# An FFT convolution with routed experts on one core: transposes as row tiles, a new order of a stage, and two moved constants

## The chip, the core and the metric

The kernel runs on one core of one Trainium2 chip. A core has TensorE (matmuls and transposes, into PSUM banks), VectorE, ScalarE, GpSimd and SyncE, which here only issues DMAs. Each engine works through a queue of its own in order. The metric is device time in microseconds of one execution; the times given are medians of runs.

## What is computed

Four sequences of 11456 rows with 128 channels go through a long convolution, done as a transform of length 5760 = 90 x 64, a product and the transform back. Each row of the result is then sent to one of eight experts.

```python
u = x * v
y = irfft(rfft(u) * rfft(filter))[:S]        # per sequence and channel
x = (x * y).reshape(B * S, D)                # 45824 rows of 128
logits = x @ w_gate + modality_bias[modality_id]
e = argmax(logits); gate = softmax(logits)[e]
out = gate * (relu(x @ w1[e]) @ w2[e])       # e of that row
```

## The kernel before

The work is a list of stages on a time line that is written out by hand. For each sequence there is an outer stage and a middle stage in turn. An outer stage has 16 steps (`q`). In one step it transforms the last sequence back (`turn`, `inverse`), routes rows of it (`half`, `logits`, `lturn`, `biased`, `choice`, `send`, `store`, `places`), and transforms the next one forward (`load`, `product`, `forward`). The middle stage multiplies the spectra. After four sequences the last outer stage has no forward part, and then the experts run, which is the second half of the time.

The string `OUTER` gives the order within a step for the first three outer stages, and a delay in steps for each part: `half:2` in step t works on q = t - 2. `LAST` is the same for the last outer stage. TensorE, ScalarE, VectorE and SyncE take their instructions in just this order. Routing parts other than `half` run in every second step, so two steps make one round: one with `lturn`, `biased` and `choice`, one with `logits` and `send`.

What the prediction's steps touch:

- `turn` (L693, L694) transposes A, [128, 90] at a time, to [90, 128]; four transposes fill a PSUM bank, and ScalarE copies the bank to `w_t`. Two blocks a step, so 16 transposes and four copies.
- `inverse` (L702 to L708): eight matmuls from `w_t` into a `pair` buffer, a copy of half of it by ScalarE (L705), then a sum, a difference and a product with x on VectorE (L706, L707, L708), which writes `xo`.
- `forward` (L494, L497): two halves of 32 matmuls in tiles of 64 x 64, each into a `pair` buffer that ScalarE copies to A. There are two `pair` buffers for `forward` and `inverse` together.
- `product` (L479, L482, L483) on VectorE makes what `forward` reads one step later.
- `half` (L751, L753): eight transposes of [109, 128] and two copies by ScalarE, for the logits (L759, L761), which `lturn` (L766) transposes back.
- `choice` (L780 to L801) on VectorE, with one exponential by ScalarE (L784): maximum, one-hot of the expert, a running count, the gate weight and the token's number. L790 adds a large constant where a position holds no row, so that no expert is chosen there.
- `send` (L819 to L833): counts by three small matmuls, then the row's place. L833 adds the same constant, so that a scatter drops the row.
- `store` (L810) writes `xo` to DRAM; there are three `xo` buffers.
- `send_rows` (L275) scatters rows by GpSimd, a few at a time, each paced by an instruction of VectorE.

Of the kernel before, what the change touches and what calls it, by code (L numbers as in the profile page):

```python
# [47 lines left out]
def surely_full(n):  # L48
# [7 lines left out]
NOWHERE = 1 << 20  # L56
OUTER = ("turn0:0 turn1:0 lturn:3 biased:3 half:2 product:0 forward:1 choice:3 "
         "inverse:0 logits:2 send:4 load_x:-1 load:-2 store:4 places:5")
# [36 lines left out]
def shape_constants():  # L95
# [32 lines left out]
    order = lambda a: a.reshape(D, 2, NO, 2, 4).transpose(0, 2, 4, 1, 3).reshape(D, NO * NC)  # L128
    first = (E - np.arange(E))[None, :, None] * np.ones((D, 1, NC))
    keep = np.ones((D, E, NC))  # L130
# [3 lines left out]
    small = np.concatenate([  # L134
        order(tok)[:, 0:NC], order(~there)[:, 0:NC] * 2.0 ** 22,
        first.reshape(D, E * NC), keep.reshape(D, E * NC), tri,
# [36 lines left out]
_at = 0  # L173
for _name, _n in (("tok", NC), ("bad", NC), ("first", E * NC), ("keep", E * NC),
                  ("tri", D), ("ones", D), ("reg", E), ("iota", NF)):
    SMALL[_name] = (_at, _at + _n)
    _at += _n
# [4 lines left out]
def hyena_moe_kernel(ctx: ExitStack, tc: tile.TileContext, a: dict, out: bass.AP,  # L182
# [24 lines left out]
    def sm(name):  # L207
        lo, hi = SMALL[name]
        return small[:, lo:hi]
# [147 lines left out]
    def first_table(new):  # L357

        n1 = new("n1", [1, E])
        dve.tensor_sub(n1, base1[0:1], reg)  # L360
        yield
        yield from floor_div(new, n1, n1, T, 0)
        yield from tile_table(new, tab1, used, reg, n1, NW1, T)
# [3 lines left out]
    with ExitStack() as cv:  # L367
# [35 lines left out]
        def split_constants():  # L403
            dve.tensor_copy(base, sm("reg"))
            dve.tensor_copy(both, small[:, SMALL["tri"][0]:SMALL["ones"][1]])
# [48 lines left out]
        def xo_of(b, o):  # L454

            return xo_t[(NO * b + o) % NXO]
# [222 lines left out]
        def inverse_stages(b):  # L679
# [8 lines left out]

            def turn(q, blk):
                for c in range(2):  # L690
                    p = bank("wt")
                    for j in range(4):
                        pe.transpose(p[0:N1, D * j:D * j + D], A[:, blk, :, 8 * q + 2 * j + c], ident)  # L693
                    act.copy(w_t[q % 2][blk][:, c], p[0:N1])  # L694

# [42 lines left out]
        def route_stages(b):  # L738
# [4 lines left out]
            fst = sm("first")[0:PU].rearrange("p (e c) -> p e c", e=E)  # L743
            bad_of = lambda o: sm("bad")

            def turn(o, half):
                xo = xo_of(b, o)
                for way in range(2):
                    pt = bank("xT")
                    for h in range(4):  # L750
                        pe.transpose(pt[:, PU * h:PU * h + PU], xo[0:PU, way, half, h, 0:D],  # L751
                                     ident[0:PU, 0:PU])
                    act.copy(xT_t[:, 2 * way + half].rearrange("p h n -> p (h n)"),  # L753
                             pt[:, 0:4 * PU])

# [19 lines left out]
            def choice(o):  # L775
# [13 lines left out]
                dve.tensor_reduce(mb, ec(sco), axis=AX.X, op=ALU.max)  # L789
                dve.tensor_add(mb, mb, bad_of(o)[0:PU])  # L790
                dve.tensor_tensor(oh[0:PU], sco, wide(mb), op=ALU.is_equal)
                dve.tensor_tensor_scan(
# [6 lines left out]
                by_h = lambda t: t.rearrange("p (h g) -> p h g", h=4)  # L799
                dve.reciprocal(xov[:, :, :, D], by_h(se))  # L800
                s = dve.tensor_scalar_add(xov[:, :, :, D + 1].bitcast(I32), by_h(sm("tok")[0:PU]),  # L801
                                          float(b * S + 8 * o))
                paced(s)

# [9 lines left out]
            def send(o):  # L814
# [12 lines left out]
                dve.tensor_add(base, base, pn)  # L827
                paced(dve.tensor_mul(ro, ro, oh[0:PU]))
                sl = rt.tile([PU, NC], F32, tag="sl", name="sl")
                dve.tensor_reduce(sl, ec(ro), axis=AX.X, op=ALU.add)  # L830
                ix = ix_t[i % 2]
                by_h = lambda t: t.rearrange("p (h g) -> p h g", h=4)
                dve.tensor_add(ix[0:PU].rearrange("p (g h) -> p h g", h=4), by_h(sl), by_h(bad_of(o)[0:PU]))  # L833

# [111 lines left out]
    def rest():  # L946


        assert not waiting
        sp.dma_start(pad, a["c_pad"].rearrange("p (j r) -> p j r", j=TH // D))  # L950
        sp.dma_start(xs[E * R:E * R + TH, :].rearrange("(p j) r -> p j r", j=TH // D), pad)
        end = new("end", [1, E], I32)
        dve.tensor_copy(end, base[0:1])
        yield
        for e in range(E):
            v = nc.values_load(
                end[0:1, e:e + 1], engines=[ENG.SP], min_val=0, max_val=E * R - TH,
                skip_runtime_bounds_check_because="a region holds every token and a tile more")
            after_all(sp.dma_start(xs[ds(v, TH), :].rearrange("(p j) r -> p j r", j=TH // D), pad),
                      scatters)  # L960
            yield

    def later_tables():

        nall, full, start, left = (new(n, [1, E]) for n in ("nall", "full", "start", "left"))
        dve.tensor_sub(nall, base[0:1], reg)
        yield
# [301 lines left out]
```

## Time and profile before

| | |
|---|---|
| time, median of 3 runs | 2077.25 us (2075.55 to 2083.45) |
| the profiled execution, its own time | 2075.4 us |
| its span, first to last instruction | 2073.5 us |
| TensorE (PE) busy | 1954.0 us, 94% |
| VectorE (DVE) busy | 1761.6 us, 85% |
| ScalarE (ACT) busy | 1277.9 us, 62% |
| GpSimd (POOL) busy | 1165.5 us, 56% |
| mean granted TensorE clock | 0.985 |

Shares are means over stages that differ: the outer stages, the middle stages and the experts have different limits. In the rows below PE is a matmul or a transpose and PEld the load of its stationary operand. A time in brackets is how long the engine stood idle ahead of the instruction, and behind the arrow is what it waited for. An entry such as x16 says that so many instructions in a row are shown as one line, with the time from the first's start to the last's end. Shapes are partitions x elements, and 64*128 in front of them is the tile of TensorE that is used. Matmul ends are modelled.

### The profile page before, as it was taken

Reading aid. Unit: us, or ns where it says so; the run is one execution under the profiler, and the core shown is the slowest. Engines: PE = TensorE matmul, PEld = TensorE weight load, DVE = VectorE, ACT = ScalarE, POOL = GpSimd, SP = SyncE. Lnnn points to the kernel's source line nnn. Section 1 sums busy time; section 2 is a strip of 40 time slices with the busy share of each in tenths; the row PEclk is TensorE's granted clock in tenths of the full one; section 3 lists DMA queues with packets and bytes.
Section 4 is the critical chain, followed back from the end, with each engine's and each line's share of the span. In section 5 each row is a group of like instructions: output and inputs, shape, how many; then the busy total and the mean of one; then the engine's idle time right before and its main releaser. Section 6 shows DMA issues by size and latency. Waiting matters only on the chain. (4 is left out here: it accounts for less than half of the span.)

```text
span 2073.5 us, 50275 instructions
## 1 busy us (share of the span) xinstructions
PE 1954.0 (94%) x17646; PEld 1549.2 (75%) x17646; DVE 1761.6 (85%) x2708; ACT 1277.9 (62%) x2372; POOL 1165.5 (56%) x1054
## 2 busy tenths in 40 slices
PE   8899898999989998999799999999999999999997
PEld 8688565776667665776477888887888888888897
DVE  6599899999999899997678988897888888888886
ACT  5555675457735675446466666665666666666675
POOL 0144004765668566974456677786556555555654
PEclk9999999999999999999899999999999999999998
DMA  8565678879988898856798466664655555555421
GB/s 320 183 190 174 232 270 263 280 265 310 331 257 260 283 334 285 280 191 175 186 248 223 90 132 136 130 125 106 116 99 96 100 97 97 97 100 98 88 44 29
DMA packets 610842, 379.47 MB, mean 183 GB/s; under 512 B 424026, under 2 KB 542005, under 8 KB 610585
## 3 DMA queue, kind: packets, MB, share of 16 engines
q1 hardware_dynamic: 587193, 328.62, 58.5%
q0 software_dynamic: 23104, 47.34, 6.6%
q8 instruction: 141, 2.31, 0.5%
q14 instruction: 116, 0.95, 0.2%
q10 hardware_dynamic: 288, 0.25, 0.1%
HBM read 272.75 MB, written 103.70 MB: 182 GB/s over the span
## 5 line engine op out<-in xcount | busy, mean ns | idle before, releaser
L1097 ACT ACTIVATE hh<-ph 128x512 fp32r<-128x512 f32 x724 | 433.6, 599 | 320.8 <-PE ph L1094 316.5
L1098 DVE SCALAR_TENSOR_TENSOR hl<-ph,hh 128x512 fp32r<-128x512 f32 x724 | 487.9, 679 | 161.3 <-ACT hh L1097 153.4
L275 POOL DMA_INDIRECT xs<-back,to x360 | 401.7, 1116 | 327.9 <-DVE se L796 109.7
L1163 POOL DMA_INDIRECT out<-ot,x x362 | 373.0, 1030 | 160.2 <-issue 36.8
L1092 PE MATMUL ph<-xh,wh 128*128 128x512 f32 (+1 forms) x792 | 297.4, 376 | 8.0 <-ACT wh L1063 8.0
L1094 PE MATMUL ph<-xl,wh 128*128 128x512 f32 (+1 forms) x792 | 296.0, 374 | 9.0 <-POOL xl L1080 9.0
L1118 PE MATMUL po<-hl,wh 128*128 128x512 f32 (+1 forms) x792 | 295.7, 373 | 1.0 <-DVE hl L1098 0.8
L1093 PE MATMUL ph<-xh,wl 128*128 128x512 f32 (+1 forms) x792 | 295.0, 373 | 0.0
L1116 PE MATMUL po<-hh,wh 128*128 128x512 f32 (+1 forms) x792 | 294.9, 372 | 0.0
L1117 PE MATMUL po<-hh,wl 128*128 128x512 f32 (+1 forms) x792 | 294.6, 372 | 0.0
L672 ACT COPY A<-pw 128x512 f32<-128x512 f32 (+1 forms) x184 | 97.1, 579 | 186.9 <-PE pw L668 186.9
L1080 POOL TENSOR_TENSOR xl<-xT,xh 128x512 fp32r<-128x512 f32 (+1 forms) x77 | 96.2, 1249 | 200.8 <-ACT xh L1076 200.8
L624 PE MATMUL pz<-A,work 128*64 128x256 f32 x1440 | 182.7, 397 | 10.4 <-DMA work<-in_c_to 7.1
L668 PEld LDWEIGHTS pw<-work 64*128 64x128 f32 x2856 | 166.3, 189 | 30.5 <-ACT work L606 19.2
L637 POOL TENSOR_TENSOR work<-work 128x512 f32<-128x512 f32 (+1 forms) x92 | 115.3, 1254 | 128.3 <-DVE work L633 127.6
L668 PE MATMUL pw<-work 64*128 64x128 f32 x2856 | 180.2, 278 | 2.9 <-POOL work L654 2.6
L1094 PEld LDWEIGHTS ph<-xl,wh 128*128 128x128 f32 x792 | 149.7, 189 | 36.9 <-POOL xl L1080 10.8
L1092 PEld LDWEIGHTS ph<-xh,wh 128*128 128x128 f32 x792 | 149.9, 189 | 33.5 <-ACT wh L1063 8.3
L1118 PEld LDWEIGHTS po<-hl,wh 128*128 128x128 f32 x792 | 149.6, 189 | 30.1 <-DVE hl L1098 4.8
L1093 PEld LDWEIGHTS ph<-xh,wl 128*128 128x128 f32 x792 | 149.9, 189 | 26.0 <-DVE wl L1064 0.4
L1117 PEld LDWEIGHTS po<-hh,wl 128*128 128x128 f32 x792 | 149.7, 189 | 25.7
L1116 PEld LDWEIGHTS po<-hh,wh 128*128 128x128 f32 x792 | 149.7, 189 | 25.3
(183 smaller groups left out, 3618.9 us busy)
## 6 DMA issues: line engine op xcount, KB each, us to landing
work<-hs SPq DMA_DIRECT2D x66, 512.0 KB
work<-in_x SPq DMA_DIRECT2D x64, 512.0 KB
work<-in_xd SPq DMA_DIRECT2D x58, 512.0 KB
work<-in_v SPq DMA_DIRECT2D x51, 512.0 KB
xr<-xo SPq DMA_DIRECT2D x64, 365.6 KB
back<-xr SPq DMA_DIRECT2D x120, 195.0 KB
work<-in_c_to SPq DMA_DIRECT2D x88, 256.0 KB
blocks<-xs SPq DMA_DIRECT2D x328, 64.0 KB
```

What stands on the lines that cost most here:

```text
L275: s = pool.indirect_dma_start(out=xs, out_offset=bass.IndirectOffsetOnAxis(ap=ix, axis=0), in_=src, in_offset=None, bounds_check=E * R - 1 ...
L624: pe.matmul(z[64 * s:64 * s + 64, t, r], k["b"][:, t, s, r], A[:, :, 4 * g + 2 * t + s], start=True, stop=True)
L668: pe.matmul(v[s][:, t, blk], k[of][at, t, r, blk], k["c"][at, t, r], start=i == 0, stop=i == len(terms) - 1)
L1092: pe.matmul(p, k[0, "h"][:, f:f + D], k["xh"], start=True, stop=False)
L1093: pe.matmul(p, k[0, "l"][:, f:f + D], k["xh"], start=False, stop=False)
L1094: pe.matmul(p, k[0, "h"][:, f:f + D], k["xl"], start=False, stop=True)
L1097: act.activation(hh, ph, AF.Relu)
L1098: steps.append(ins_of(dve.scalar_tensor_tensor(hl, ph, 0.0, hh.bitcast(F32), op0=ALU.max, op1=ALU.subtract)))
L1116: pe.matmul(po, k[1, "h"][:, f], hh[:, t], start=g == 0, stop=False)
L1117: pe.matmul(po, k[1, "l"][:, f], hh[:, t], start=False, stop=False)
L1118: pe.matmul(po, k[1, "h"][:, f], hl[:, t], start=False, stop=g == NCH - 1)
L1163: s = pool.indirect_dma_start(out=out, out_offset=bass.IndirectOffsetOnAxis(ap=ix, axis=0), in_=src, in_offset=None, bounds_check=N - 1, o ...
```

## The change

`turn` and `half` do each transpose in two: the upper 64 partitions and the rest, each in a row tile of TensorE of its own and into a PSUM bank of its own. A block now has 16 transposes of [64, 90] and a bank for each of the two tiles; the two copies by ScalarE take one bank each, that is, half of the columns of all results instead of all columns of half of them. `half` has 16 transposes, of 64 and 45 partitions.

In `OUTER`, `product` and `forward` come right behind the turns; `half` follows, and `lturn`, `biased` and `choice` come behind `half` instead of ahead of it. `LAST` stays.

A position without a row now has zeros in the constant `first`, and the comparison takes at least 0.5, so that nothing is chosen there: L790 and the constant `bad` go. The base of all places starts at 2^22 (`FAR`) and the chosen expert's place is that less 2^22, so that a minimum over the experts gives the place and, where none is chosen, a number beyond the end: L833 goes, and the reduction writes the place itself. Token numbers are written by ScalarE instead of L801.

```diff
@@ -54,7 +54,8 @@
 NH = (N - T * NF - E) // TH + E
 RW = D + 2
 NOWHERE = 1 << 20
-OUTER = ("turn0:0 turn1:0 lturn:3 biased:3 half:2 product:0 forward:1 choice:3 "
+FAR = float(1 << 22)
+OUTER = ("turn0:0 turn1:0 product:0 forward:1 half:2 lturn:3 biased:3 choice:3 "
          "inverse:0 logits:2 send:4 load_x:-1 load:-2 store:4 places:5")
 LAST = ("inverse:1 logits:3 turn0:0 half:2 lturn:3 turn1:0 biased:4 choice:4 load_x:-1 store:4 "
         "send:5 places:5")
@@ -126,13 +127,13 @@
     win = win.reshape(2, 64, 2, N2).transpose(2, 1, 3, 0)
 
     order = lambda a: a.reshape(D, 2, NO, 2, 4).transpose(0, 2, 4, 1, 3).reshape(D, NO * NC)
-    first = (E - np.arange(E))[None, :, None] * np.ones((D, 1, NC))
+    first = (E - np.arange(E))[None, :, None] * order(there * 1.0)[:, None, 0:NC]
     keep = np.ones((D, E, NC))
     keep[:, :, 0] = 0
     q, p = np.arange(D)[:, None], np.arange(D)[None, :]
     tri = np.concatenate([-(q >= p).astype(float), np.ones((D, D))], 1)
     small = np.concatenate([
-        order(tok)[:, 0:NC], order(~there)[:, 0:NC] * 2.0 ** 22,
+        order(tok)[:, 0:NC],
         first.reshape(D, E * NC), keep.reshape(D, E * NC), tri,
         np.ones((D, 1)) * (np.arange(E) * R)[None, :],
         np.ones((D, 1)) * np.arange(NF)[None, :],
@@ -171,7 +172,7 @@
 
 SMALL = {}
 _at = 0
-for _name, _n in (("tok", NC), ("bad", NC), ("first", E * NC), ("keep", E * NC),
+for _name, _n in (("tok", NC), ("first", E * NC), ("keep", E * NC),
                   ("tri", D), ("ones", D), ("reg", E), ("iota", NF)):
     SMALL[_name] = (_at, _at + _n)
     _at += _n
@@ -357,7 +358,7 @@
     def first_table(new):
 
         n1 = new("n1", [1, E])
-        dve.tensor_sub(n1, base1[0:1], reg)
+        dve.scalar_tensor_tensor(n1, base1[0:1], -FAR, reg, op0=ALU.add, op1=ALU.subtract)
         yield
         yield from floor_div(new, n1, n1, T, 0)
         yield from tile_table(new, tab1, used, reg, n1, NW1, T)
@@ -401,7 +402,7 @@
                          .partition_broadcast(D).rearrange("p (m e) -> p m e", m=2))
 
         def split_constants():
-            dve.tensor_copy(base, sm("reg"))
+            dve.tensor_scalar_add(base, sm("reg"), FAR)
             dve.tensor_copy(both, small[:, SMALL["tri"][0]:SMALL["ones"][1]])
 
         pool.memset(wg, 0.0)
@@ -687,11 +688,16 @@
                 sp.dma_start(t, a["x"][b, q])
 
             def turn(q, blk):
+                p = [bank("wt")[0:N1].rearrange("p (i d) -> p i d", d=64) for _ in range(2)]
                 for c in range(2):
-                    p = bank("wt")
                     for j in range(4):
-                        pe.transpose(p[0:N1, D * j:D * j + D], A[:, blk, :, 8 * q + 2 * j + c], ident)
-                    act.copy(w_t[q % 2][blk][:, c], p[0:N1])
+                        for k in range(2):
+                            at = slice(64 * k, 64 * k + 64)
+                            pe.transpose(p[k][:, 4 * c + j], A[at, blk, :, 8 * q + 2 * j + c],
+                                         ident[at, at])
+                w = w_t[q % 2][blk].rearrange("p c (j k d) -> p (c j) k d", k=2, d=64)
+                for k in range(2):
+                    act.copy(w[:, :, k], p[k])
 
             def transform(q):
 
@@ -741,17 +747,19 @@
             ec = lambda t: t.rearrange("p e c -> p c e")
             wide = lambda t: t.unsqueeze(1).broadcast_to([PU, E, NC])
             fst = sm("first")[0:PU].rearrange("p (e c) -> p e c", e=E)
-            bad_of = lambda o: sm("bad")
 
             def turn(o, half):
                 xo = xo_of(b, o)
+                rows = (slice(0, 64), slice(64, PU))
+                pt = [bank("xT")[:, 0:8 * (at.stop - at.start)].rearrange("p (w h n) -> p w h n", w=2, h=4)
+                      for at in rows]
                 for way in range(2):
-                    pt = bank("xT")
                     for h in range(4):
-                        pe.transpose(pt[:, PU * h:PU * h + PU], xo[0:PU, way, half, h, 0:D],
-                                     ident[0:PU, 0:PU])
-                    act.copy(xT_t[:, 2 * way + half].rearrange("p h n -> p (h n)"),
-                             pt[:, 0:4 * PU])
+                        for p, at in zip(pt, rows):
+                            pe.transpose(p[:, way, h], xo[at, way, half, h, 0:D], ident[at, at])
+                xT = xT_t.rearrange("p (w s) h n -> p w s h n", w=2)[:, :, half]
+                for p, at in zip(pt, rows):
+                    act.copy(xT[:, :, :, at], p)
 
             def logits(o):
                 pl = bank("pl")
@@ -787,8 +795,8 @@
                 dve.scalar_tensor_tensor(sco, dl, 0.0, fst, op0=ALU.is_ge, op1=ALU.mult)
                 mb = rt.tile([PU, NC], F32, tag="mb", name="mb")
                 dve.tensor_reduce(mb, ec(sco), axis=AX.X, op=ALU.max)
-                dve.tensor_add(mb, mb, bad_of(o)[0:PU])
-                dve.tensor_tensor(oh[0:PU], sco, wide(mb), op=ALU.is_equal)
+                dve.scalar_tensor_tensor(oh[0:PU], sco, 0.5, wide(mb), op0=ALU.max,
+                                         op1=ALU.is_equal)
                 dve.tensor_tensor_scan(
                     sc[0:PU].rearrange("p e c -> p (e c)"), sm("keep")[0:PU],
                     oh[0:PU].rearrange("p e c -> p (e c)"), 0.0, op0=ALU.mult, op1=ALU.add)
@@ -797,10 +805,9 @@
                 dve.tensor_scalar_add(se, se, 1e-9)
                 xov = xo[0:PU].rearrange("p w s h r -> p h (w s) r")
                 by_h = lambda t: t.rearrange("p (h g) -> p h g", h=4)
-                dve.reciprocal(xov[:, :, :, D], by_h(se))
-                s = dve.tensor_scalar_add(xov[:, :, :, D + 1].bitcast(I32), by_h(sm("tok")[0:PU]),
-                                          float(b * S + 8 * o))
-                paced(s)
+                act.activation(xov[:, :, :, D + 1].bitcast(I32), by_h(sm("tok")[0:PU]), AF.Copy,
+                               bias=float(b * S + 8 * o))
+                paced(dve.reciprocal(xov[:, :, :, D], by_h(se)))
 
             def store(o):
                 xo = xo_of(b, o)
@@ -825,12 +832,10 @@
                 ro = rt.tile([PU, E, NC], F32, tag="ex", name="ro", bufs=1)
                 dve.tensor_add(ro, prv[0:PU], base[0:PU].unsqueeze(2).broadcast_to([PU, E, NC]))
                 dve.tensor_add(base, base, pn)
-                paced(dve.tensor_mul(ro, ro, oh[0:PU]))
-                sl = rt.tile([PU, NC], F32, tag="sl", name="sl")
-                dve.tensor_reduce(sl, ec(ro), axis=AX.X, op=ALU.add)
+                paced(dve.scalar_tensor_tensor(ro, oh[0:PU], -FAR, ro, op0=ALU.mult, op1=ALU.add))
                 ix = ix_t[i % 2]
-                by_h = lambda t: t.rearrange("p (h g) -> p h g", h=4)
-                dve.tensor_add(ix[0:PU].rearrange("p (g h) -> p h g", h=4), by_h(sl), by_h(bad_of(o)[0:PU]))
+                dve.tensor_reduce(ix[0:PU].rearrange("p (g h) -> p h g", h=4),
+                                  ro.rearrange("p e (h g) -> p h g e", h=4), axis=AX.X, op=ALU.min)
 
             def places(o):
                 ix = ix_t[(b * NO + o) % 2]
@@ -950,7 +955,7 @@
         sp.dma_start(pad, a["c_pad"].rearrange("p (j r) -> p j r", j=TH // D))
         sp.dma_start(xs[E * R:E * R + TH, :].rearrange("(p j) r -> p j r", j=TH // D), pad)
         end = new("end", [1, E], I32)
-        dve.tensor_copy(end, base[0:1])
+        dve.tensor_scalar_add(end, base[0:1], -FAR)
         yield
         for e in range(E):
             v = nc.values_load(
@@ -963,7 +968,7 @@
     def later_tables():
 
         nall, full, start, left = (new(n, [1, E]) for n in ("nall", "full", "start", "left"))
-        dve.tensor_sub(nall, base[0:1], reg)
+        dve.scalar_tensor_tensor(nall, base[0:1], -FAR, reg, op0=ALU.add, op1=ALU.subtract)
         yield
         yield from floor_div(new, full, nall, T, 0)
         dve.tensor_sub(full, full, used)
```

## Rows read from the trace of the kernel before

**Rows 1.** Stretches: us; busy of PE, PEld, DVE, ACT, POOL; PEclk; DMA share, GB/s.

```profile
218.00:340.00 122.00, 113.12 (x1665) 77.00 (x1664) 112.45 (x215) 86.30 (x162) 8.32 (x8) 1.00 0.74 253
260.80:319.50 58.70, 55.96 (x832) 38.43 (x830) 56.37 (x117) 42.83 (x82) 0.00 (x0) 1.00 0.78 266
```

**Rows 2.** In order of time, a pair of steps (start, us, engine; idle before).

```profile
260.78 1.23 DVE L708 TENSOR_TENSOR xo<-work 128x1024 f32<-128x1024 f32 x1
...
269.73 0.69 DVE L707 TENSOR_TENSOR work<-py,work 128x512 f32<-128x512 f32 x1
...
270.47 0.85 PE L494 MATMUL s<-fwd,work 64*64 64x90 f32 x32 [0.33 <-DVE work L707]
...
273.24 0.58 ACT L705 COPY work<-py 128x512 f32<-128x512 f32 x1 [1.09 <-PE py L702]
...
274.05 0.68 DVE L706 TENSOR_TENSOR work<-py,work 128x512 f32<-128x512 f32 x1
...
275.50 1.23 DVE L708 TENSOR_TENSOR xo<-work 128x1024 f32<-128x1024 f32 x1
```

**Rows 3.** In order of time, first steps of the first outer stage.

```profile
236.56 1.94 PE L702 MATMUL py<-work,inv 90*64 90x512 f32 x8 [0.26 <-ACT A L497]
...
239.19 0.69 DVE L706 TENSOR_TENSOR work<-py,work 128x512 f32<-128x512 f32 x1 [1.15 <-ACT work L705]
...
242.85 1.94 PE L702 MATMUL py<-work,inv 90*64 90x512 f32 x8 [0.27 <-ACT A L497]
```

**Rows 4.** In order of time, last outer stage (SPq: SyncE's queue issues).

```profile
937.47 1.09 ACT L694 COPY work<-wt 90x512 f32<-90x512 f32 x2
...
979.53 1.76 SPq L810 DMA_DIRECT2D xr<-xo  x2
...
987.73 1.23 DVE L708 TENSOR_TENSOR xo<-work 128x1024 f32<-128x1024 f32 x1 [2.96 <-DMA xr<-xo]
```

**Rows 5.** In order of time, `send` and `choice` of that pair.

```profile
262.63 0.38 DVE L830 TENSOR_REDUCE sl<-ro 109x16 f32<-109x128 f32 x1
...
263.05 0.19 DVE L833 TENSOR_TENSOR ix<-sl,small 109x16 int32<-109x16 f32 x1
...
266.58 0.31 ACT L784 ACTIVATE ex<-lg 109x128 f32<-109x128 f32 x1 [1.24 <-DVE lg L782]
...
267.31 0.18 DVE L790 TENSOR_TENSOR mb<-mb,small 109x16 f32<-109x16 f32 x1
...
269.00 0.12 DVE L801 TENSOR_SCALAR xo<-small 109x16 int32<-109x16 f32 x1
```

**Rows 6.** In order of time, weight loads (PEld) before and in an outer stage.

```profile
201.41 1.87 PEld L668 LDWEIGHTS pw<-back,work 64*128 64x128 f32 x32
...
252.31 1.81 PEld L693 LDWEIGHTS wt<-ident,A 128*90 128x90 f32 x16 [0.81 <-issue]
...
254.05 0.81 PEld L751 LDWEIGHTS xT<-ident,xo 109*128 109x128 f32 x8
...
255.00 1.29 PEld L494 LDWEIGHTS s<-fwd,work 64*64 64x64 f32 x64
```

**Rows 7.** Groups by line and form, loads, whole span (busy us, mean ns).

```profile
L668 PEld LDWEIGHTS pw<-work 64*128 64x128 f32 x2856 | 166.3, 189 | 30.5 <-ACT work L606 19.2 <-POOL work L654 4.0 <-issue 3.4
...
L693 PEld LDWEIGHTS wt<-ident,A 128*90 128x90 f32 x1024 | 117.6, 183 | 41.2 <-issue 15.3 <-PE py L702 9.7 <-DVE lg L782 7.3
...
L494 PEld LDWEIGHTS s<-fwd,work 64*64 64x64 f32 x3264 | 67.8, 133 | 23.0 <-DVE work L707 7.9 <-ACT A L497 6.2 <-issue 2.5
...
L751 PEld LDWEIGHTS xT<-ident,xo 109*128 109x128 f32 x512 | 52.1, 142 | 10.7 <-ACT work L761 4.2 <-issue 4.1
```

**Rows 8.** In order of time, a stand of TensorE early in the first outer stage.

```profile
229.49 0.85 PE L494 MATMUL s<-fwd,work 64*64 64x90 f32 x32 [1.80 <-DVE work L707]
```

**Rows 9.** Stretches as in rows 1, right behind the first outer stage.

```profile
344.60:347.50 2.90, 0.04 (x2) 0.00 (x0) 2.83 (x4) 0.00 (x0) 1.61 (x3) 1.00 0.47 157
347.50:354.00 6.50, 4.00 (x19) 1.95 (x19) 6.22 (x13) 2.60 (x5) 3.36 (x4) 0.51 0.90 264
```

## The prediction

> **What bounds the kernel now.** I read the table of stretches first, for one outer stage and for the even middle of it [rows 1]. There TensorE works 55.96 of 58.7 us and VectorE 56.37, so both look full, and the share of busy time does not say which of them sets the pace. ScalarE has 16 us to spare. GpSimd and the DMA share may be left aside, since VectorE has no DMA wait in the rows of the loop [rows 2].
>
> Next I read that stretch in order of time [rows 2]. Two steps of the loop (one with `choice`, one without; I call them a pair) last from one L708 at 260.78 to the next but one at 275.50: 14.7 us. In that pair VectorE goes from one instruction to the next. The idle time that the table leaves it, 0.58 us in a pair, is the small gaps between short dependent operations. TensorE stands once, for 0.33 us: the second half of `forward` (L494 at 270.47) waits for L707, which ends at 269.73 + 0.69 = 270.42. The reason is in the code: `forward` and `inverse` share two `pair` buffers in turn, so the second half of `forward` needs the buffer that the inverse before it filled, and L707 is its last reader. So from the fifth step of an outer stage on VectorE sets the pace, and TensorE is just behind.
>
> The first steps have no `choice` and no `send`. There an inverse follows the last after 242.85 - 236.56 = 6.29 us, and VectorE waits 1.15 us of that for ScalarE's copy of the inverse [rows 3]. Its own work is thus 5.14 us, and TensorE is the bound.
>
> The last outer stage has another order, which isn't changed. There VectorE's L708 stands 2.96 us for the store of an older `xo` buffer [rows 4]; the store was issued at 979.53 and L708 starts at 987.73, 8.2 us later.
>
> **VectorE's edits.** L790 (0.18 us), L833 (0.19) and L801 (0.12) go [rows 5]. L801 depends on neither neighbour and can overlap them, so between 0 and its 0.12 I count 0.05. The other replaced operations keep shape and engine, and I take them as equal. That is 0.42 us for each `choice` with its `send`, bounds 0.37 and 0.49. A stage has eight; seven lie where VectorE sets the pace, so -2.9 us a stage (bounds -2.5 and -3.5). The token write on ScalarE comes behind L784, which takes 0.31 us for eight times as many elements and had waited 1.24 us for VectorE; ScalarE's spare time covers it, so 0. Without that cover it would cost at most that 0.31.
>
> **TensorE's edits.** Loads show the rate. Sixteen transposes of `turn` need (1.81 - 0.183) / 15 = 0.108 us each, eight of `half` (0.81 - 0.142) / 7 = 0.095 [rows 6, 7]. The nearest rows for two half-height tiles at once are L668's: 32 loads of 64 x 128 in 1.87 us, (1.87 - 0.189) / 31 = 0.054 us each, so two tiles do run side by side. That is 0.108 for a pair of tiles that stream 128 columns; the new transposes stream 64, which gives 0.054 for a pair if streaming is the limit. The other bound is today's single transpose, 0.108 and 0.095, in which the same load is hidden. Between them I go by the load: 64 columns take 133 ns and 128 take 189, or 0.875 ns more per column, so 90 columns are an estimated 0.079 us. A `turn` pair at 0.079 makes both turns 16 x 0.079 = 1.26 us instead of 1.73. The load of `half` is a short one (142 ns for 128 columns), so I take 0.07 between its bounds: 8 x 0.07 = 0.56 us instead of 0.76, bounds 0.43 and 0.76.
>
> The Trainium skill's page "TensorE: Matmul & The Clock Gate", section "LDWEIGHTS (loading the stationary operand)", says that a load takes its columns divided by 1.2 in ns, which is 107 ns for the 128 columns of `half`. The trace has such loads each 95 ns, so the measurement decides; by the page `half` would take 0.86 us, and the predicted time would be some 4.5 us longer.
>
> A change of tile shape costs too. L751's loads begin 0.07 us before L693's have ended (252.31 + 1.81 against 254.05: one shape), while L494's begin 0.14 after L751's (254.86 against 255.00: another shape) [rows 6]. The new order has two more such changes a step; each 0.1 us, bounds 0 and 0.2.
>
> **The order.** What counts is what stands between that wait for L707 and the next L706. Before, only half of `forward` and the inverse do: from 270.42 to the end of L705 at 273.24 + 0.58 = 273.82 is 3.40 us [rows 2]. VectorE comes to L706 at 274.05, after 3.63 us, so the chain is hidden with 0.23 to spare. In the new order `half` lies behind `forward` on TensorE's queue, so it waits for L707 as well, and the inverse behind it. `lturn` does too, but in the step with `choice`, where VectorE has three microseconds more. The chain becomes 3.40 + 0.56 + 0.1 = 4.06 us, and VectorE, whose work up to L706 is unchanged, now waits 4.06 - 3.63 = 0.43 us (bounds 0.20 and 0.73) in each step without `choice`. Five of these in a stage: +2.2 us (+1.0 to +3.7). So the wait gives back most of what VectorE saves.
>
> In the first steps the same chain closes: 4.06 us, then L706 and L707, 275.50 - 274.05 - 0.04 = 1.41, makes 5.47 us instead of 6.29 (bounds 5.24 and 5.77). Only the steps with `half` and without `choice` gain, two a stage: -1.6 us (-2.1 to -1.0). The faster turns are worth nothing beyond that: from the fifth step they only make TensorE stand longer.
>
> One stage: -2.9 + 2.2 - 1.6 = -2.3 us (bounds -4.6 and +0.2). Three stages: -6.9 (-13.8 to +0.6).
>
> **The last outer stage** has the new `turn` without the new order. There the inverse of a step runs right behind its turns and ScalarE's copies: two of L694 at 937.47 take 1.09 us [rows 4]. Today the first inverse matmuls of a block need one of the two; with copies by halves of the columns they need both, 0.54 us more. The first copy also has to wait for eight pairs (0.63 us) instead of four transposes (0.43): 0.2. In the four steps ahead of the first wait for a store that is +3.0 us (0 to +4, since TensorE may catch up). From there the wait for the store covers it, and that loop gets shorter by the 0.23 us that `choice` sheds, five times: -1.1. Together +1.9 (-1.1 to +3).
>
> **Sum.** -6.9 + 1.9 = -5.0 us on the profiled execution's 2075.4: 2070.4. The median of the runs is 1.85 us above that execution, so I say 2071.
>
> **Rivals.** (1) *The clock falls; slower.* TensorE's one stand of 0.33 us grows by what it sheds in a pair, 2 x (0.47 + 0.20), and by `half` and a change moved behind the wait, 0.66; four changes take 0.4 off: 1.9 us. It stood 1.80 us ahead of 229.49 [rows 8] and the stage kept its granted clock of 1.00, the 2.4 GHz level [rows 1]; after 344.60 it did nearly nothing for 2.9 us, and the next stretch shows 0.51, mostly the 1.2 GHz level [rows 9]. What 1.9 us does no row says. At half clock the 2.7 us of `forward`, `half` and inverse behind the wait take some 2 us longer, and VectorE waits for all of it. Nine falls among the fifteen stands make the kernel slower than no change by over 0.5%; twelve give 2071 + 24 = 2095. For it: the stand is at the edge. Against: any slower transpose shortens it. Chance 0.17.
>
> (2) *The tiles do not overlap as transposes.* Then 32 x 0.079 = 2.53 us for the turns, 1.12 for `half`, 0.2 for changes: +1.36 a step, of which 0.7 a pair is covered (14.7 less 14.0 us of work [rows 1]); with five and a half pairs and three first steps +15 us a stage, 2118. At 0.054 each it is about +3 a stage, 2080. Against: L668's matmuls overlap. Chance 0.10.
>
> (3) *The wait does not appear; faster.* If `half` is at its lower bound and the second half of `forward` gets a buffer earlier, VectorE's saving counts in full: -3.4 - 2.1 = -5.5 us a stage, and none of the last stage's loss: 2075.4 + 1.85 - 16.5 = 2061. Chance 0.20.
>
> **The numbers.** The forecast has 0.53 and a range of its own of 2064 to 2079. No change is 2077; 0.5%, about what a measurement of this kernel tells from nothing, is 10.4 us, so the bounds are 2067 and 2087.5. Faster: all of (3) and a fifth of the forecast, 0.3. Slower: two thirds each of (1) and (2), 0.18. The rest, 0.52, is within. The range takes in (3) and its own looseness, and most of (1): 2056 to 2094.
>
> **What would show it.** In the outer stages L693's loads in pairs and both turns in about 1.3 us; a wait of L706 for L705 of some 0.4 us in every second step, where there is none; TensorE's stand ahead of L494 of near 2 us; pairs still at about 14.7; an inverse each 5.5 us in the first steps; the granted clock at 1.00. The prediction is wrong if pairs come to 14.2 (no wait), if the clock shows 0.5 inside an outer stage, if a pair of tiles takes over 0.108 us, or if the last stage loses more than 4 us.

## The result and the profile after

The changed kernel takes 2104.14 us (median of 6 runs, 2100.75 to 2115.42) against 2077.6 (also of six): ratio 1.0135, 95% interval 1.0119 to 1.0151, so it is slower by 1.35%. I had said 2071 and a range up to 2094.

The profiled execution is the longest of the six, 2115.42 us with a span of 2113.7, so I compare it by stages and not in sum, and its last stage may be longer than usual. Lines have moved by up to 8; L714 is the old L708, L712 the old L706, L495 the old L494.

First the stretch of the outer stage that answers to the second of [rows 1], from L714 to the eighth L714 behind it (us; busy of PE, PEld, DVE, ACT, POOL; granted clock; DMA share, GB/s):

```profile
261.19:320.81 59.62, 54.80 (x1021) 37.08 (x1020) 55.49 (x104) 44.29 (x85) 0.00 (x0) 1.00 0.77 263
```

Four pairs of steps take 59.62 us and not 58.71; the clock is 1.00. The same pair as in [rows 2] and [rows 6] in order of time shows where:

```profile
261.19 1.24 DVE L714 TENSOR_TENSOR xo<-work 128x1024 f32<-128x1024 f32 x1
...
267.30 1.73 PEld L696 LDWEIGHTS wt<-ident,A 64*90 64x90 f32 x32 [0.81 <-issue]
...
270.48 1.23 DVE L714 TENSOR_TENSOR xo<-work 128x1024 f32<-128x1024 f32 x1
...
270.59 0.85 PE L495 MATMUL s<-fwd,work 64*64 64x90 f32 x32 [0.64 <-DVE work L713]
...
271.37 0.58 PEld L759 LDWEIGHTS xT<-ident,xo 64*128 64x128 f32 x16
...
274.61 0.70 DVE L712 TENSOR_TENSOR work<-py,work 128x512 f32<-128x512 f32 x1 [0.45 <-ACT work L711]
...
276.07 1.23 DVE L714 TENSOR_TENSOR xo<-work 128x1024 f32<-128x1024 f32 x1
```

The first step, with `choice`, takes 9.29 us, the second, without it, 5.59 (before 9.67 and 5.05). The forecast wait for ScalarE's copy is there: 0.45 us, where I had worked out 0.43. In the first steps an L714 follows the last after 5.74 us (241.59 to 247.33, the answer to [rows 3]), not 6.29. So the three outer stages are nearly even: from the second L708 to the sixteenth they take 100.03, 99.64 and 100.62 us, before 100.10, 100.13 and 100.55.

Two things in the outer stages I had not forecast. In each step with `choice` TensorE issues one transpose of the second turn and then stands 0.57 us for a PSUM bank that ScalarE is still copying. And in the very first step of the first outer stage the granted clock is 0.50 from 223.4 to 230.2 us: the inverse there takes 4.65 us, and the first two products into `xo` lie 5.79 us apart, not 4.97. From 235 us on it is 1.00 in all three outer stages.

```profile
223.26 4.65 PE L708 MATMUL py<-work,inv 90*64 90x512 f32 x8 [0.36 <-ACT work L700]
...
261.81 1.04 PE L696 MATMUL wt<-ident,A 64*90 64x64 f32 x15 [0.57 <-ACT work L700]
```

The last outer stage is another matter. The stretch from its first L708 (L714) to its sixteenth, columns as above, before and then after:

```profile
927.76:1019.16 91.40, 85.08 (x566) 55.17 (x564) 65.52 (x157) 56.15 (x116) 42.12 (x41) 1.00 0.62 173
```

```profile
932.71:1055.86 123.15, 114.72 (x898) 55.64 (x899) 64.47 (x141) 59.81 (x120) 39.94 (x42) 0.76 0.49 133
```

It takes 31.75 us more, of the 40.0 by which the two profiled executions differ, and its mean granted clock is 0.76: nearly half of it ran at the 1.2 GHz level. It also begins 4.95 us later, 2.4 us of them between the third outer stage's last product and its own first, and the experts behind it take 3.5 us more (1057.8 us; in all the kernels profiled here 1053.3 to 1059.3). What lies between the outer stages I did not follow.

TensorE alone in that stage of the kernel after, in order of time, and then two stretches cut where the clock changes:

```profile
976.35 1.04 PE L696 MATMUL wt<-ident,A 64*90 64x64 f32 x16
977.23 0.22 PE L759 MATMUL xT<-ident,xo 64*128 64x64 f32 x1
978.06 0.69 PE L759 MATMUL xT<-ident,xo 45*128 45x45 f32 x15 [0.61 <-ACT work L700]
978.55 0.31 PE L696 MATMUL wt<-ident,A 64*90 64x64 f32 x1
979.45 1.04 PE L696 MATMUL wt<-ident,A 64*90 64x64 f32 x15 [0.59 <-ACT work L762]
980.42 4.80 PE L708 MATMUL py<-work,inv 90*64 90x512 f32 x8
985.15 1.68 PE L767 MATMUL pl<-work,wg 128*32 128x436 f32 x8
```

```profile
976.00:981.00 5.00, 3.80 (x51) 2.72 (x50) 3.75 (x7) 3.31 (x7) 1.94 (x2) 1.00 0.63 183
981.00:988.00 7.00, 7.00 (x40) 2.19 (x40) 4.07 (x12) 2.04 (x7) 1.94 (x3) 0.51 0.67 179
```

Two things are to be seen in these rows. `half` issues one transpose and then stands 0.61 us; the second turn issues one and stands 0.59 us. One transpose, because a group of row tiles opens two PSUM banks with its first two instructions, and the second bank isn't free. Then the clock drops, the inverse takes 4.80 us and the logits (L767) 1.68. In the kernel before the same place looks like this, with 0.94 us for the logits (L759) and 2.16 for the inverse:

```profile
974.74 0.94 PE L759 MATMUL pl<-work,wg 128*32 128x436 f32 x8
975.61 1.13 PE L693 MATMUL wt<-ident,A 128*90 128x128 f32 x8
976.58 0.54 PE L751 MATMUL xT<-ident,xo 109*128 109x109 f32 x4
978.35 0.59 PE L751 MATMUL xT<-ident,xo 109*128 109x109 f32 x4 [1.23 <-ACT work L761]
978.82 0.69 PE L766 MATMUL lt<-ident,work 128*109 128x128 f32 x4
979.35 1.09 PE L693 MATMUL wt<-ident,A 128*90 128x128 f32 x8
...
980.50 2.16 PE L702 MATMUL py<-work,inv 90*64 90x512 f32 x8
```

There the stand is as long, 1.23 us in one piece, and the clock stays at 1.00.

### The profile page after: what moved, and what is told of

Its sections match the earlier page's. It is cut to its first block, busy times and chain, and to the rows that moved or that the text cites. A ratio compares the mean times of both kernels' runs of the same rounds, so it can differ in the third digit from the quotient of the medians.

```text
span 2113.7 us, 53058 instructions
## 1 busy us (share of the span) xinstructions
PE 1984.6 (94%) x19182; PEld 1544.6 (73%) x19182; DVE 1755.4 (83%) x2612; ACT 1292.1 (61%) x2404; POOL 1166.1 (55%) x1054
## 5 line engine op out<-in xcount | busy, mean ns | idle before, releaser
L1099 PEld LDWEIGHTS ph<-xl,wh 128*128 128x128 f32 x792 | 150.4, 190 | 36.9 <-POOL xl L1085 10.6
```

Of the source, the lines that this page charges most:

```text
L1099: pe.matmul(p, k[0, "h"][:, f:f + D], k["xl"], start=False, stop=True)
```

## The experiments

Each ratio is to the kernel before, measured beside it. "Stage" is the last outer stage, from its first product into `xo` to its sixteenth.

**The last stage with its old turns (last_old).**

```diff
 def turn(q, blk):
+    if b == nb - 1:
+        for c in range(2):
+            p = bank("wt")
+            for j in range(4):
+                pe.transpose(p[0:N1, D * j:D * j + D], A[:, blk, :, 8 * q + 2 * j + c], ident)
+            act.copy(w_t[q % 2][blk][:, c], p[0:N1])
+        return
```

`half` gets its old form in the same way.

> The changed kernel, but the last outer stage makes both its turns and `half` as before (128 and 109 rows at once); everything else stays changed. Theory: the loss lies in that stage alone and comes from the turns there, because TensorE's granted clock falls to the 1.2 GHz level in it. Then the clock shows 1.00 in that stage, two steps take about 12.8 us (13.0 less the 0.23 that `choice` sheds) instead of 17.1, and the kernel takes 2075, between 2068 and 2080. Rival: the stage is slower because the token numbers are now written by ScalarE behind its other copies, which lets the stores go later; then two steps stay at 17 us and the kernel near 2100.

2078.29 us, ratio 0.9992 (0.9982 to 1.0001).

```profile
934.25:1023.65 89.40, 84.86 (x566) 55.16 (x564) 63.28 (x140) 56.74 (x122) 42.08 (x41) 1.00 0.65 176
```

The stage takes 89.40 us at a clock of 1.00, 2.0 less than before, and all the loss is gone. ScalarE's token numbers are still there, so the rival falls. The time is 3 us above what I expected, inside the range given: the rest of the change is worth nothing, not a gain.

**The late copies alone (last_waits).** All eight transposes of a block, of 128 rows, then the two copies, the one needed first last:

```diff
+    p = [bank("wt") for _ in range(2)]
...
+    for c in (1, 0):
+        act.copy(w_t[q % 2][blk][:, c], p[c][0:N1])
```

> As the kernel with the old turns in the last stage, but there all eight transposes of a block come ahead of its two copies, and the copy that the first inverse matmuls need comes second. So the inverse waits for all copies, as it does behind the row tiles, while TensorE does the transposes with 128 rows. Theory (the tiles): the waits alone cost a few tenths of a us in the first steps and are covered later; the clock stays at 1.00 in the stage, and the kernel takes up to 4 us more than with the old turns, 2075 to 2080. Rival (the waits): the stands ahead of the inverse are what lowers the clock; then the stage shows stretches at 0.50 and the kernel takes 2095 or more.

2090.65 us, ratio 1.0047 (1.0029 to 1.0064).

```profile
930.27:1031.88 101.61, 96.91 (x564) 53.13 (x565) 64.16 (x141) 58.38 (x122) 39.94 (x42) 1.00 0.59 157
```

```profile
969.00 0.59 PE L765 MATMUL xT<-ident,xo 109*128 109x109 f32 x4 [0.35 <-ACT work L697]
969.35 1.24 DVE L722 TENSOR_TENSOR xo<-work 128x1024 f32<-128x1024 f32 x1
...
970.55 1.07 PE L716 MATMUL py<-work,inv 90*64 90x512 f32 x2
971.83 1.93 PE L716 MATMUL py<-work,inv 90*64 90x512 f32 x6 [0.21 <-ACT work L697]
```

Neither theory. The clock keeps its 1.00, as the first said, but the waits cost 12.2 us and not up to 4: two steps take 14.0 us instead of some 12.6. They aren't covered: the product into `xo` (L722, the old L708) no longer waits for a store, for which it stood 2.96 us in [rows 4], so that cover is used up (VectorE stands 11.4 us for stores in this stage in `last_old`, and not at all here), and TensorE with ScalarE's copies sets the pace. The turns hold their banks longer here too, and `half` waits 0.35 us for one.

**More work ahead of the inverse (last_filled).**

```diff
 py = pair("py")
+if b == nb - 1:
+    pe.matmul(py[0:64, 0], inv[:, 0], small[0:N1, 0:512], start=True, stop=True)
```

> The changed kernel with more work: in the last stage each inverse has one more matmul of 90 x 64 by 512 columns ahead of it, on constants, whose result is written over. It takes 0.48 us at the 2.4 GHz level and stands where TensorE waits for the copies. Theory: the stage is long only by the clock, and the clock falls because TensorE has too little to do there with row tiles; then the clock stays at 1.00 for most of the stage, two steps take 13 to 14 us, and the kernel is faster than the changed one by 15 to 28 us (2076 to 2089) in spite of the work added. Rival: TensorE's queue itself has become the limit of the stage; then each of sixteen steps takes 0.5 to 1.0 us more and the kernel 2112 to 2120.

2106.52 us, ratio 1.0123 (1.0102 to 1.0145).

```profile
927.95:1047.54 119.59, 111.02 (x939) 62.32 (x938) 64.49 (x141) 60.25 (x121) 39.93 (x42) 0.83 0.49 134
```

A miss on both sides. With some 7 us of work added (15 by 0.48) the profiled stage is 3.6 us shorter and its mean clock 0.83 instead of 0.76, but it still falls. By the medians the two kernels don't differ, and the changed one's profile is its longest run, so the 3.6 us are no gain that is shown. The matmul stands ahead of the inverse, and the two stands of 0.6 us for the banks come earlier in the step.

**VectorE's edits alone (vector_only):** the constants, the base of the places and ScalarE's token numbers, on the kernel before.

> The kernel before with the edits on VectorE alone (positions without a row in the constants, the base of the places, token numbers by ScalarE); old turns, old order. Theory of the prediction: VectorE sets the pace from the fifth step of an outer stage on, so a pair of steps takes 14.66 less 0.42, about 14.25 us, and nothing is given back, since `half` stays ahead of `forward`. That is 2.9 us a stage in three stages and about 1.1 us in the last: 2077.5 less 9.8, about 2067 (2064 to 2071). Rival: the pair loses only about 0.2 us, as what is removed overlapped its neighbours or TensorE's chain takes over; then the kernel takes 2072 or more.

2071.54 us, ratio 0.9966 (0.9954 to 0.9978), -7.1 us. A pair takes 14.32 us (its L709 is the old L708):

```profile
261.18 1.23 DVE L709 TENSOR_TENSOR xo<-work 128x1024 f32<-128x1024 f32 x1
...
275.50 1.23 DVE L709 TENSOR_TENSOR xo<-work 128x1024 f32<-128x1024 f32 x1
```

That is 0.34 to 0.40 us off a pair: the price of the removed instructions was right, the sum of 9.8 us too high.

**The new order too (vector_order):** `vector_only` with the new `OUTER`, turns as before.

> VectorE's edits and the new order of the first three outer stages, all turns and `half` as before. Theory: what the three outer stages lose against VectorE's edits alone is the order: `half` with 0.9 us (instead of 0.7) stands between TensorE's wait and the inverse, so the wait of the first subtraction for ScalarE's copy is some 0.6 us in each step without `choice`, against 0.45 with row tiles; pairs of steps take about 15.0 us (14.87 with row tiles, 14.36 with VectorE's edits alone) and the kernel 2079, between 2076 and 2082. Rival: the row tiles are what costs there; then pairs take 14.4 and the kernel 2071.

2082.1 us, ratio 1.0017 (1.0000 to 1.0033): the order alone costs 10.6 us. Its wait is here, 0.70 us behind the longer `half` (L707 is the old L706):

```profile
278.98 0.70 DVE L707 TENSOR_TENSOR work<-py,work 128x512 f32<-128x512 f32 x1 [0.70 <-ACT work L706]
```

**Row tiles in the old order (vector_tiles):** `vector_only` with the new turns and `half` in the first three outer stages.

> VectorE's edits and row tiles in the first three outer stages, in the old order; the last stage has its old turns. Theory: without the order the row tiles cost nothing there and gain only in the first two steps with `half` and without `choice`, where TensorE's work sets the pace: some 0.2 us each; pairs stay at 14.36 and the kernel takes 2070, between 2067 and 2073. Rival: the tiles cost by themselves, by the copies that come later or by the clock in TensorE's longer stands; then 2076 or more.

2094.58 us, ratio 1.0069 (1.0053 to 1.0085). The rival holds. In the old order the two turns, `lturn` and `half` come one behind the other and share four banks; two steps take 15.5 us, and the step without `choice` 6.25 of them, against 5.59 in the changed kernel:

```profile
264.01 1.13 PE L703 MATMUL wt<-ident,A 64*90 64x64 f32 x17
265.71 1.03 PE L703 MATMUL wt<-ident,A 64*90 64x64 f32 x15 [0.57 <-ACT work L707]
...
273.97 0.70 PE L775 MATMUL xT<-ident,xo 45*128 45x45 f32 x15 [0.20 <-ACT work L707]
...
276.57 1.94 PE L715 MATMUL py<-work,inv 90*64 90x512 f32 x8 [0.51 <-ACT A L498]
```

The stand of 0.57 us between the turns is there in both orders, so it is not what the order changes. Two other waits are. `half` waits 0.20 us for a bank, and the inverse 0.51 us (0.22 in `vector_only`) for ScalarE's copy of `forward`, which comes behind the two late copies of `half`. In the changed kernel's steady steps neither wait is there. So the new order isn't only a cost: it puts `forward`, which uses other banks, between the turns and `half`. This is read from the rows; no run tests it by itself. The clock plays a part too: the third outer stage here has a fall, and two steps of 9.34 and 12.0 us in it.

**Four copies of half size (last_tiles_early):**

```diff
 for c in range(2):
...
-for k in range(2):
-    act.copy(w[:, :, k], p[k])
+    for k in range(2):
+        act.copy(w[:, 4 * c:4 * c + 4, k], p[k][:, 4 * c:4 * c + 4])
```

> The changed kernel, in whose last stage ScalarE copies each bank of a row tile in two halves: four copies of 256 columns a block instead of two of 512, the first two of them behind the first eight transposes. So the first inverse matmuls no longer need the last copy, and the tiles stay. Theory (waits and tiles together): with the old turns the stage takes 89.4 us, with the waits alone 101.6 at the full clock, with waits and row tiles 123.2 at a falling clock; without the waits TensorE is busy more densely and the clock falls less: the kernel takes 2082 to 2092. Rival (tiles alone lower the clock): the falls stay, 2095 or more. Second rival (the waits alone): nothing is left of the loss, 2076 to 2080.

2136.28 us, ratio 1.0282 (1.0261 to 1.0303).

```profile
926.36:1070.97 144.61, 125.43 (x912) 62.26 (x910) 64.83 (x141) 66.21 (x180) 39.96 (x42) 0.58 0.42 113
```

The clock is at its lower level for five sixths of the stage. It doesn't show what it was made for, since the edit brings a wait of its own: the second eight transposes of a turn go into the banks that ScalarE is copying, and TensorE stands for that in each turn:

```profile
971.83 0.69 PE L698 MATMUL wt<-ident,A 64*90 64x64 f32 x8
972.97 0.89 PE L698 MATMUL wt<-ident,A 64*90 64x64 f32 x8 [0.45 <-ACT work L701]
```

A bank is also still held from the first transpose to its last copy. So TensorE stands 2.6 us in a round of two steps, in six pieces of 0.35 to 0.63, instead of 1.2 us in two. It shows that the earlier copies don't help in this form, and not what they would do without the new stands.

**One kind of row tile at a time.** First the turns alone, with the old `half` (last_turn_tiles):

> The changed kernel, in whose last stage `half` alone is as before (eight transposes of 109 rows); the turns there keep row tiles and their late copies. Theory: the turns' 32 transposes of a step, not the 16 of `half`, are what lowers the clock on top of the waits; the stage shows stretches at 0.50 and the kernel takes 2097 to 2105. Rival: both kinds are needed for it; then the clock is at 1.00 in the stage, which takes about 101 us as with the waits alone, and the kernel 2088 to 2092.

2092.95 us, ratio 1.0060 (1.0039 to 1.0080).

```profile
931.29:1034.31 103.02, 100.23 (x788) 54.59 (x789) 64.12 (x141) 58.17 (x122) 39.96 (x42) 1.00 0.57 155
```

Then `half` alone, with the old turns (last_half_tiles):

> The changed kernel, in whose last stage the turns are as before (128 rows, copies by halves of the columns' sets) and only `half` uses row tiles: the other half of the run in which only the turns did. Theory: neither kind alone lowers the clock; `half` has to find two free banks at once and waits some 0.3 to 0.6 us in a step, which the wait for the stores covers in part: clock 1.00 in the stage, 89 to 96 us for it, kernel 2078 to 2085. Rival: the small transposes of `half` lower the clock by themselves; then 2092 or more, with stretches at 0.50.

2077.9 us, ratio 0.9994 (0.9980 to 1.0008).

```profile
926.38:1016.78 90.40, 86.38 (x686) 54.01 (x684) 63.37 (x141) 58.82 (x122) 42.04 (x41) 1.00 0.66 175
```

Neither lowers the clock in this stage by itself. The turns cost what the late copies cost (103.0 against 101.6), `half` 1.0 us; both together 33.8 us, of which the last 20 (some 15 by the ratios) come with the falls of the clock. But neither run has the two stands of 0.6 us either: in a round of the first TensorE waits 0.20 us for a bank, and in the second it waits in three rounds only, 0.17 to 0.72 us for `half`.

**Two more banks (last_more_banks).** In the last stage there is no `forward`, so one of the two `pair` buffers can serve `half`:

```diff
+apart = pair("py") if b == nb - 1 else None
-pt = [bank("xT")[:, 0:8 * (at.stop - at.start)].rearrange("p (w h n) -> p w h n", w=2, h=4)
-      for at in rows]
+pt = [(bank("xT") if apart is None else apart[:, i])[:, 0:8 * (at.stop - at.start)]
+      .rearrange("p (w h n) -> p w h n", w=2, h=4) for i, at in enumerate(rows)]
```

> The changed kernel, in whose last stage the two banks of `half` come from the `pair` buffers, which only the inverse uses there, instead of from the four banks that turns, logits and counts share. Tiles, late copies and order stay. Theory (banks): a row-tile group opens two banks at once and frees them at its end, so with four banks in all TensorE stops after one transpose of `half` for 0.61 us and after one of the second turn for 0.59; with two more banks these stands go, the clock stays at 1.00 in the stage, the stage takes 95 to 102 us instead of 123.2, and the kernel 2078 to 2086. Rival: the late copies and the small tiles are enough for the falls; then stretches at 0.50 remain, and the kernel takes 2097 or more.

2086.22 us, ratio 1.0033 (1.0021 to 1.0045).

```profile
934.47:1031.77 97.30, 92.88 (x909) 49.62 (x910) 63.96 (x141) 59.56 (x121) 39.51 (x42) 0.96 0.60 162
```

```profile
971.30 1.04 PE L696 MATMUL wt<-ident,A 64*90 64x64 f32 x16
972.18 0.66 PE L760 MATMUL py<-ident,xo 64*128 64x64 f32 x16
972.68 1.39 PE L696 MATMUL wt<-ident,A 64*90 64x64 f32 x16
973.99 1.07 PE L708 MATMUL py<-work,inv 90*64 90x512 f32 x2
975.50 1.93 PE L708 MATMUL py<-work,inv 90*64 90x512 f32 x6 [0.43 <-ACT work L700]
```

Same tiles, same late copies, same order: both stands of 0.6 us are gone, and with them 25.9 of the 33.8 us in the stage, or, by the ratios of the whole kernels, 21.2 of 29.7. Of the 25.9, 20.6 lie in the last eleven of the fifteen steps, where those stands were. One fall is left, near 928 to 942, in the first steps; from there the clock is 1.00 and two steps take 13.05 us. What stays is the late copy, 0.43 us ahead of the other inverse matmuls.

**One instruction less (vector_more):** `vector_only` without `dve.tensor_scalar_add(se, se, 1e-9)`, which leaves out an addition that a 32-bit sum of 1 or more can't show.

> VectorE's edits alone (old turns, old order), less one more instruction of 0.17 us in each `choice`: the addition of 1e-9 to a sum of exponentials of which one is 1, which a 32-bit float can't show. Theory: VectorE still sets the pace, so a pair of steps goes from 14.36 to some 14.2 us: -0.17 in 7 pairs of three stages, with the last stage some 4 us, and the kernel takes 2067.5 (2065 to 2070), 0.995 of before. Rival: TensorE's chain behind L707 now closes and nothing is gained: 2071, 0.9965.

2069.4 us, ratio 0.9953 (0.9936 to 0.9970), the lowest of all. In the steady pairs the rival holds; 261.63 to 275.94 is 14.31 us, as without the edit, because TensorE's chain now closes:

```profile
274.48 0.70 DVE L707 TENSOR_TENSOR work<-py,work 128x512 f32<-128x512 f32 x1 [0.23 <-ACT work L706]
```

The 0.0013 between it and `vector_only` are not clear of noise: the two intervals overlap.

## Why the prediction was wrong

By ratios, in us of the kernel before: VectorE's edits -7.1, the order +10.6, row tiles in the first three outer stages in that order -5.2 (`last_old` against `vector_order`), row tiles in the last stage +29.7; together +28.0. They are differences between one kernel and the next, so they add up by construction; each carries an uncertainty of some 3 to 4 us.

**VectorE's edits: the price right, the count high.** Forecast -8.7 us in three stages and -1.1 in the last, measured -7.1 in all. I counted seven rounds in each stage. The trace of `vector_only` has the saving in the steady pairs, but none in the first pair with `choice` (13.88 us against 13.87), and its three outer stages are 1.7, 0.0 and 1.3 us shorter from their second product to the sixteenth.

**The order: the mechanism right.** The wait was put at 0.43 us and is 0.45. One price was missing in the steps with `choice`: `biased` now stands directly ahead of the reduction that needs it, and the next instruction starts after 0.32 us (265.81 to 266.13). In `vector_only` the independent product L480 stands between them and starts after 0.20 us (277.64 to 277.84).

```profile
265.81 0.28 DVE L780 TENSOR_TENSOR lg<-lt,bs 109x128 f32<-109x128 f32 x1
...
266.13 0.37 DVE L788 TENSOR_REDUCE mx<-lg 109x16 f32<-109x128 f32 x1
```

So a pair comes to 14.88 us, not 14.7, and the three outer stages to -0.5 us (from their second step on) instead of -6.9, inside the bounds that I gave for them.

**The rate of the turns: near its upper bound.** 32 loads take 1.73 us; with one load at 0.21 a pair takes (1.73 - 0.21) / 15 = 0.101 us, where one load of 128 rows took 0.108 and I chose 0.079. So the turns gain little on TensorE, the first steps come to 5.74 and not 5.5 us, and the stand ahead of the second half of `forward` is 0.64 and not 1.9. `half` came out near its price: its 16 loads take 0.58 us, by the same working (0.58 - 0.146) / 7 = 0.062 for a pair, where I had 0.07. Why the turns' pairs are the slower ones was not tested; the columns that `turn` loads from A lie 128 numbers apart, those of `half` side by side.

**The last outer stage: the step that failed.** It reads: "Together +1.9 (-1.1 to +3)". It measured +31.75 us in the profiled execution. I priced the late copies, 0.54 and 0.2 us, in four steps and let the wait for the stores cover the rest. Two things were wrong. The cover is thinner than the waits: the late copies alone add 12.2 us at the full clock (`last_waits`), 0.9 to 1.0 us in each of the first three steps, where I had 0.74, and 1.4 in each steady round, where I had nothing. And I counted the banks of a group one after the other, as the code before uses them. The four that turns, `half`, logits and counts share are mentioned nowhere in my working. A group of row tiles needs two at once and holds both to its end; with `half` in two banks of its own the stage is 25.9 us shorter, and nothing else is changed. The clock's falls are in that number, and not all of them are due to the banks.

**The clock: the right rival, mostly in the wrong place.** I put it at the stand ahead of the second half of `forward`, where it stays at 1.00. But 0.50 inside an outer stage was one of my signs of being wrong, and it is there, in the first step of the first one. Eight of the nine profiled kernels with row tiles in that stage have such a fall there, the four without have none, and in the kernel after no stand for a bank is near it. So the tiles, or the late copies that come with them, seem to matter there without the banks. This is not tested, and the ninth, `last_tiles_early`, runs the same code at 1.00.

In the last stage the falls are of two kinds. The first fall is the longest. Here is its stretch in the kernel after, and then the same stretch in `last_turn_tiles`:

```profile
926.60:957.30 30.70, 30.15 (x201) 14.33 (x201) 13.17 (x22) 12.59 (x25) 7.13 (x8) 0.50 0.20 66
```

```profile
926.60:957.30 30.70, 29.62 (x237) 16.03 (x237) 16.24 (x26) 17.11 (x34) 8.90 (x9) 1.00 0.30 97
```

It holds 24.6 of the stage's 58 us at the lower level, and costs some 6 us in the first four steps (31.25 us against 25.09). It begins before `half` does and well before the stage's first stand for a bank, which ends at 963.49, so the banks don't explain it. `last_turn_tiles` has the same instructions up to `half` and no fall, `last_more_banks` has a shorter one; its cause stays open.

The other kind are the five falls from 981 us on. Each begins 1.4 to 1.8 us after the second of the two stands for banks has ended (979.45 and 981.2, 996.58 and 998.2, and so on), though not every such pair is followed by one. Without the row tiles of either kind, or with two more banks, these stands go, and the steady steps run at 1.00. That these falls follow from the stands is shown from three sides. What is not shown is what the clock looks at, and whether the small tiles are needed: 1.23 us of standing between transposes of 128 rows leaves it alone, and so does one stand of 0.57 us in a round between half-height ones, in the outer stages; two of 0.6 us in a round don't. No run here separates their length, their number and the tiles.

## What to carry to other kernels

When one group of instructions is split over two buffers that are open at the same time, count the buffers of the pool first: who holds how many, from which instruction to which, and in every stage that calls the code, also one whose order the change leaves alone. A stage without the work that elsewhere stands between the groups is where it shows most. And a cover of 2.96 us for a wait is used up by several small waits in the same step: add up all the new ones before calling one hidden.

## What the runs showed of the hardware

A pair of half-height transposes takes nearly as long to load as one of full height (0.101 us against 0.108 for 90 columns); the pair with 128 columns in `half` is quicker, 0.062 us against 0.095. Added work need not cost time where the clock falls: one more matmul in each step, 7 us in sum, left the kernel no slower (2106.52 against 2104.14 us, with overlapping intervals). And one and the same code can have a fall of the clock in one execution and none in another, as the first step of the first outer stage shows: 4.65 us for its inverse in the kernel after, 2.90 in `last_tiles_early`.
